# A start-up plan with four places for raw weights, exponentials with running sums on ScalarE, and new planned durations

## The chip, the cores and the metric

The kernel runs on one core of one Trainium2 chip. The metric is the device time of one execution in microseconds (us), as the median of several runs. The profile is of one execution of its own.

## The reference, cut to what matters

Everything is float32 on the inputs' side; the weights arrive as float64 words and are converted on the chip.

```python
# attention in chunks of 32 queries, with 8 memory keys, 16 keys to the left, 8 to the right
scores = scale * np.matmul(q_c, k_full.transpose(0, 1, 3, 2))
scores = scores - np.max(scores, axis=-1, keepdims=True)
a = np.exp(scores)
a = a / (np.sum(a, axis=-1, keepdims=True) + 1e-09)
out[:, :, c_start:c_end] = np.matmul(a, v_full)
...
x = attn_out.transpose(0, 2, 1, 3).reshape(3072, 512)
h = x @ w_in                                  # w_in 512 x 2048
x = (h * (1.0 / (1.0 + np.exp(-1.702 * h)))) @ w_out
h = x @ w_in2
out = (np.maximum(h, 0.0) + alpha * np.minimum(h, 0.0)) @ w_out2
```

## The kernel before, in words

Attention's output is cut into six blocks of 512 tokens. For each block, the first gated layer runs over 16 chunks of 128 hidden units: a product `h` (`mm1`, 12 matmuls of 128x512), a tanh on ScalarE and a multiplication on VectorE (`act1`), a split of the result into a high and a low part (`split_g`, ScalarE then VectorE), and a product into the block's output `ya`/`yb` (`mm2_t`, 12 matmuls). Every matmul operand stands as a high and a low part, so each product is three matmuls. The second layer follows from about 600 us on, and the change does not touch its code.

The change lies in the **start**: block 0. Here three kinds of work run together.

- *First steps* `m` = 0 to 3 (`a_load` ... `a_xpart`): attention for 128 tokens each. TensorE makes the scores `sc`, VectorE the maximum `mx`, the difference, the sum `sm` and the division, ScalarE the exponential between them; then TensorE transposes (`pt`), ScalarE copies (`p`), TensorE multiplies with `v` (`xp`), ScalarE and VectorE write the high and low parts of the block's input `x`.
- *Weights*: 16 chunks of the first layer. `w_load` fetches a chunk's raw words in two DMAs of 512 KB into a tile `wraw`; `w_abs` (ScalarE, L107), `w_bits` 0 to 3 (VectorE, L115, L117, L121, L125), `w_high` (ScalarE, `whi`, L134) and `w_low` (VectorE, `wlo`, L139) turn it into the matmul's two parts. The tile `wtmp` between them has two buffers, so `w_abs` of a chunk waits for `w_low` of the chunk two before it.
- *Double steps* 4 and 6 (`d_load` ... `d_xcopy`): attention for 256 tokens each, for the next block. Their exponentials are already 16 activations of 64 columns with the sum as accumulator (`d_exp`, L414).

What order these have on each engine is set by `emit_jobs`: each piece of work is a `job` with an engine, a planned duration, a rank and its dependencies. A list scheduler takes, again and again, the job that can start earliest (rank decides between equals), and the program is then written out in order of planned start; `keep_in_program_order` (`kp`) fixes that order on every engine and in SyncE's DMA queue. So planned durations are not run times: they decide only who stands before whom. `T_LAND` is what the plan adds after a load, `T_SEM` between engines.

Memory limits the raw weights: before, chunks 0, 1 and 3 to 15 share two places in the pool `wr`, and chunk 2 has one place in the pool `start`. A load of a chunk from 5 on waits until the last reading step (`w_bits` 3, L125) of the chunk two before it is done; chunks 3 and 4 wait for the chunk three before.

Of the kernel before, what the change touches and what calls it, by code (L numbers as in the profile page):

```python
# [56 lines left out]
def fused_kernel(ctx: ExitStack, tc: tile.TileContext, qs, ks, vs, ident, w_in1, w_out1, w_in2, w_out2, alpha, out):  # L57
# [26 lines left out]
    kp = tc.keep_in_program_order  # L84

    def chunk_pool(f):
        return wp if f < NLEFT else side["wp"]

    def w_load(f, half):
        if half == 0:  # L90
            pool = side["start"] if f == 2 else wr
            wst[f] = [pool.tile([128, 2, 512, 2], U32, tag="wraw", name=f"wraw{f}", bufs=1 if f == 2 else 2), None]
        t = wst[f][0]
        if half == 0:
            kp(nc.sync.dma_start(
                out=t[:, 0].rearrange("p n t -> p (n t)").rearrange("p (k f) -> p k f", k=NKC),
                in_=w_in1.bitcast(U32)[:, f * 256:(f + 1) * 256].rearrange("(k p) f -> p k f", p=128),
            ))
        else:
            kp(nc.sync.dma_start(  # L100
                out=t[:, 1].rearrange("p n t -> p (n t)"), in_=w_out1.bitcast(U32)[f * 128:(f + 1) * 128, :],
            ))
# [788 lines left out]

    def emit_jobs():

        free = dict.fromkeys(("pe", "v", "s", "q"), 0.0)
        lag = {"q": T_LAND}
        todo = list(jobs)
        out = []
        while todo:
# [12 lines left out]
        for _, _, j in sorted(out, key=lambda o: o[:2]):  # L911
            j["fn"](*j["args"])
# [56 lines left out]
    for u, m in enumerate((4, 6)):  # L969
        r = DRANK[u]  # L970
        for k, c in enumerate((1.34, 2.2, 2.7)):
            free_ = {0: f"dp{m - 2}", 1: f"dt{m - 2}", 2: f"dp{m - 2}"}[k]
            job(f"dl{m}{k}", "q", c, LOAD_RANK["d"] + 100 * u + k, [free_, f"lv{NSTART - 1}"], d_load, m, k)
        job(f"ds{m}", "pe", 1.5, r, [f"dl{m}0", f"dl{m}1", f"dw{m - 2}1", f"su{NSTART - 2}", f"m1{0}"], d_scores, m)
        job(f"dm{m}", "v", 1.5, r, [f"ds{m}"], d_max, m)
        for k in range(4):
            job(f"de{m}{k}", "s", 1.05, r + 10, [f"dm{m}" if k == 0 else f"de{m}{k - 1}"], d_exp, m, k)
# [3 lines left out]
        job(f"dp{m}", "pe", 2.0, r, [f"dc{m}", f"dl{m}2"], d_pv, m)  # L981
# [93 lines left out]
```

## Time and profile before

| what | value |
|---|---|
| median of 3 runs | 1102.36 us (1102.33 to 1103.25) |
| the profiled execution's own time | 1103.58 us |
| its span, first to last instruction | 1101.8 us |
| mean granted TensorE clock | 0.995 of full speed |
| busy over the span | TensorE 97%, VectorE 69%, ScalarE 37% |
| DMA | 200.22 MB, mean 182 GB/s |

The span is what the trace shows; 1.8 us lie outside it. Busy shares are means over very different stretches. In the page's picture of 40 equal slices, the first slice (27.5 us) has TensorE busy for six tenths, the next three for eight, and nearly all the rest for nine tenths or more. So the start is read by itself, with stretches, waits and engines in order of time. A wait is put down to whatever came last; "issue" is time in which the engine waited for nothing that the profile shows. PE is TensorE, DVE VectorE, ACT ScalarE, SP SyncE, which issues the loads.

### The profile page before, as it was taken

What the parts mean: (1) busy time and instruction counts of PE and PEld (TensorE: products, weight loads), DVE (VectorE), ACT (ScalarE), POOL (GpSimd) and SP (SyncE); (2) the same over time, 40 slices, a digit from 0 to 9 for tenths busy, and PEclk for the clock granted to TensorE, in tenths of its full rate; (3) what the DMA queues carried; (4) which work ended last, traced back from release to release, by engine and by line L of the source; (5) the groups of instructions that cost most, each with busy time, mean ns of one, the idle gap of its engine ahead of it and who ended that gap; (6) DMA issues with size and microseconds to landing.
All of it is one profiled execution on the core that took longest, in us unless ns stands there. A gap on an engine that the chain in (4) does not pass through costs nothing.

```text
span 1101.8 us, 18264 instructions
## 1 busy us (share of the span) xinstructions
PE 1069.9 (97%) x7516; PEld 871.8 (79%) x7516; DVE 762.8 (69%) x1034; ACT 405.1 (37%) x613; POOL 0.2 (0%) x4
## 2 busy tenths in 40 slices
PE   6888999999999999999999999999999999999998
PEld 5776778788888888788778888888888888888886
DVE  6898852667666766666662257798767888677965
ACT  3555432334444343344432222155222345122442
POOL 0000000000000000000000000000000000000000
PEclk9998999999999999999999999999999999999999
DMA  9474612254745555554351066676666867666661
GB/s 350 149 242 146 210 40 90 100 199 158 253 169 208 189 210 194 182 209 157 126 164 65 1 189 189 210 271 211 201 200 194 298 198 220 198 188 214 218 202 58
DMA packets 83619, 200.22 MB, mean 182 GB/s; under 512 B 9041, under 2 KB 25809, under 8 KB 83537
## 3 DMA queue, kind: packets, MB, share of 16 engines
q1 hardware_dynamic: 83536, 199.07, 54.5%
q8 instruction: 59, 0.97, 0.4%
q14 instruction: 24, 0.19, 0.1%
HBM read 157.10 MB, written 41.94 MB: 181 GB/s over the span
## 4 chain that ended last, share of the span: by engine, by line
PE 84%; DVE 7%; DMA 4%; ACT 2%; issue 2%; SPq 1%; DVEq 0%; ACTq 0%
PE h L509 19%; PE accx L810 15%; PE accx L712 12%; PE ya L572 10%; PE yb L572 10%; PE accy L810 6%; PE accy L712 6%; PE hz L712 3%; DMA wraw<-w_out 2%; PE xp L452 1%; PE sc L374 1%; PE pt L436 1%; DVE wtmp L121 1%; DMA k<-ks 1%; DVE wlo L139 1%
## 5 line engine op out<-in xcount | busy, mean ns | idle before, releaser
L509 PE MATMUL h<-x,whi 128*128 128x512 f32 x768 | 242.9, 398 | 3.3 <-ACT whi L134 1.6
L509 PEld LDWEIGHTS h<-x,whi 128*128 128x128 f32 x768 | 145.4, 190 | 36.3 <-ACT whi L134 2.2
L523 DVE SCALAR_TENSOR_TENSOR t<-t,h 128x512 f32<-128x512 f32 x96 | 65.8, 686 | 146.4 <-ACT t L518 146.4
L509 PE MATMUL h<-x,wlo 128*128 128x512 f32 x384 | 152.4, 397 | 2.3 <-DVE wlo L139 2.3
L518 ACT ACTIVATE t<-h 128x512 f32<-128x512 f32 x96 | 57.2, 596 | 169.2 <-PE h L509 169.2
L509 PEld LDWEIGHTS h<-x,wlo 128*128 128x128 f32 x384 | 73.1, 190 | 20.1 <-DVE wlo L139 4.1
L810 PE MATMUL accx<-r,u 128*128 128x512 f32 x360 | 86.5, 396 | 0.0
L564 DVE TENSOR_TENSOR gl<-t,gh 128x512 fp32r<-128x512 f32 x96 | 66.1, 688 | 29.5 <-ACT gh L558 29.5
L712 PE MATMUL accx<-xw,u 128*128 128x512 f32 x240 | 85.8, 390 | 0.3 <-ACT u L695 0.3
L810 PE MATMUL accx<-rx,u 128*128 128x512 f32 x360 | 84.6, 391 | 0.0
L810 PEld LDWEIGHTS accx<-r,u 128*128 128x128 f32 x360 | 67.6, 188 | 16.2
L558 ACT CAST gh<-t 128x512 fp32r<-128x512 f32 x96 | 59.7, 622 | 56.1 <-DVE t L523 52.5
L572 PE MATMUL ya<-gl,whi 128*128 128x512 f32 x192 | 76.5, 398 | 3.4 <-DVE gl L564 3.4
L572 PE MATMUL ya<-gh,whi 128*128 128x512 f32 x192 | 78.4, 408 | 1.3 <-ACT gh L558 1.1
L810 PEld LDWEIGHTS accx<-rx,u 128*128 128x128 f32 x360 | 67.4, 188 | 15.0 <-DVE rx L765 0.5
L572 PE MATMUL yb<-gh,whi 128*128 128x512 f32 x192 | 76.1, 396 | 1.0 <-ACT o L581 0.9
L572 PE MATMUL ya<-gh,wlo 128*128 128x512 f32 x192 | 76.0, 396 | 0.0
L572 PE MATMUL yb<-gl,whi 128*128 128x512 f32 x192 | 75.7, 394 | 0.0
L572 PE MATMUL yb<-gh,wlo 128*128 128x512 f32 x192 | 75.6, 394 | 0.0
L695 ACT COPY s<-accx 128x512 f32<-128x512 f32 x24 | 14.1, 589 | 148.3 <-PE accx L712 148.3
L761 ACT CAST rx<-g 128x1024 fp32r<-128x1024 f32 x42 | 44.3, 1055 | 64.5 <-DVE g L542 24.3
L712 PE MATMUL accx<-xh,u 128*128 128x512 f32 x192 | 67.0, 390 | 0.0
(147 smaller groups left out, 1798.1 us busy)
## 6 DMA issues: line engine op xcount, KB each, us to landing
u<-wo SPq DMA_DIRECT2D x84, 512.0 KB, 4.7
u<-wi SPq DMA_DIRECT2D x72, 512.0 KB, 4.2
v<-vs SPq DMA_DIRECT2D x10, 1024.0 KB, 7.6
k<-ks SPq DMA_DIRECT2D x10, 832.0 KB, 5.3
wraw<-w_in SPq DMA_DIRECT2D x16, 512.0 KB, 5.2
wraw<-w_out SPq DMA_DIRECT2D x16, 512.0 KB, 5.6
raw<-w_in SPq DMA_DIRECT2D x32, 256.0 KB, 3.9
wi<-ob SPq DMA_DIRECT2D x16, 512.0 KB, 4.1
```

The costliest lines, as they stand in the source:

```text
L121: kp(nc.vector.scalar_tensor_tensor(out=a, in0=top, scalar=0xC0000000, in1=a, op0=ALU.bitwise_and, op1=ALU.bitwise_or))
L139: kp(nc.vector.tensor_tensor(out=l, in0=af, in1=h.bitcast(F32), op=ALU.subtract))
L509: pe(nc.tensor.matmul(h[:, :n], w[:, 0, k * 128:(k + 1) * 128], x[:, z, k, :n], start=(i == 0), stop=(i == 3 * NKC - 1)))
L518: mark["s"] = pin(nc.scalar.activation(out=t, in_=h, func=AF.Tanh, scale=1.702 / 2)).ins
L523: mark["v"] = pin(nc.vector.scalar_tensor_tensor(out=t, in0=t, scalar=1.0, in1=h, op0=ALU.add, op1=ALU.mult)).ins
L558: mark["s"] = pin(nc.scalar.copy(gh, g)).ins
L564: mark["v"] = pin(nc.vector.tensor_tensor(out=gl, in0=g, in1=gh.bitcast(F32), op=ALU.subtract)).ins
L572: pe(nc.tensor.matmul(y[m][:, :n], w[:, 1, m * 128:(m + 1) * 128], g[:, :n], start=(f == 0 and i == 0), stop=(f == NF - 1 and i == 2),))
L695: kp(nc.scalar.copy(t, src))
L712: kp(nc.tensor.matmul(to, w[:, c, k * 128:(k + 1) * 128], x[:, k], start=(i == 0 and n not in ADDED), stop=(i == 5), skip_group_check=n in ...
L761: kp(nc.scalar.copy(ring[P, d, jj][0], src))
L810: kp(nc.tensor.matmul(to[:, m], w[:, ft, c, m * 128:(m + 1) * 128], g[:, ft], start=(jj == 0 and ft == 0 and i == 0 and n not in ADDED), s ...
```

## The change

- **Four places.** Chunks 0 to 13 use four places: `f % 4` of 0 or 1 in `wr`, of 2 or 3 in a new pool `boost`. A load waits for the chunk four before it. Chunks 14 and 15 go to `wr` and wait for the chunk two before.
- **Pools.** `start` (the first steps' tiles) is closed after step 3 by a new job `open`; its memory then holds the converted chunks 10 to 13 (`wpb`) and the double steps' tiles. So the double steps' loads wait for the end of the first steps. `boost` is closed at chunk 14, where its memory becomes `wp2`.
- **Exponentials.** `a_sub` and `a_sum` (VectorE) are gone. ScalarE scales the maximum once (`nmx`) and makes 8 activations of 64 columns each, with `nmx` as bias and the sum as accumulator.
- **Durations, ranks, dependencies.** New planned durations, a later `T_LAND`, dependencies looked up when the plan is made, and rank 39 on TensorE for the double steps' scores, transposes and products, ahead of rank 40 of the `y` products.

```diff
-T_LAND = 2.2
-T_SEM = 0.12
-LOAD_RANK = dict(q0=0, q1=1, id=2, v0=3, w0=4, ... w2=11, d=130)
-DRANK = (95, 150)
+T_LAND = 2.7
+T_SEM = 0.15
+LOAD_RANK = dict(q0=0, q1=1, id=2, v0=3, w0=4, ... w2=11, w3=12, d0=105, d1=145)
+DRANK = (110, 160)
...
     def chunk_pool(f):
-        return wp if f < NLEFT else side["wp"]
+        return wp if f < NLEFT else side["wp"] if f >= NF - 2 else side["wpb"]
...
-            pool = side["start"] if f == 2 else wr
-            wst[f] = [pool.tile([128, 2, 512, 2], U32, tag="wraw", name=f"wraw{f}", bufs=1 if f == 2 else 2), None]
+            pool = side["boost"] if f < NF - 2 and f % 4 >= 2 else wr
+            wst[f] = [pool.tile([128, 2, 512, 2], U32, tag="wraw", name=f"wraw{f}", bufs=2), None]
...
-    def a_sub(m):
-        t["ex"] = side["start"].tile([128, 2, 4, KW], F32, tag="ke", name=f"ex{m}", bufs=NSTART)
-        kp(nc.vector.tensor_tensor(out=t["ex"], in0=t["sc"], in1=spread(t["mx"]), op=ALU.subtract))
-    def a_exp(m):
-        kp(nc.scalar.activation(out=ex, in_=ex, func=AF.Exp, scale=1.0 / D ** 0.5))
-    def a_sum(m):
-        kp(nc.vector.tensor_reduce(
-            out=t["sm"].rearrange("p (z n) -> p z n", z=2), in_=t["ex"], axis=mybir.AxisListType.X, op=ALU.add
-        ))
+    def a_exp(m):
+        t = st[m]
+        nmx = side["start"].tile([128, 2 * HP], F32, tag="nmx", name=f"nmx{m}", bufs=2)
+        kp(nc.scalar.mul(nmx, t["mx"], -1.0 / D ** 0.5))
+        t["ex"] = side["start"].tile([128, 2, 4, KW], F32, tag="ke", name=f"ex{m}", bufs=NSTART)
+        for i in range(2 * HP):
+            kp(nc.scalar.activation(
+                out=t["ex"][:, i // 4, i % 4], in_=t["sc"][:, i // 4, i % 4], func=AF.Exp, scale=1.0 / D ** 0.5,
+                bias=nmx[:, i:i + 1], accum_out=t["sm"][:, i:i + 1],
+            ))
...
-    side["start"] = side_stack.enter_context(tc.tile_pool(name="start", bufs=1, side="right"))
-    att_open("at", 1)
+    side["boost"] = side_stack.enter_context(tc.tile_pool(name="boost", bufs=2, side="right"))
+    start_stack = ExitStack()
+    side["start"] = start_stack.enter_context(tc.tile_pool(name="start", bufs=1))
+    def start_done():
+        start_stack.close()
+        side["wpb"] = ctx.enter_context(tc.tile_pool(name="wpb", bufs=1))
+        att_open("at", 1)
...
-        job(f"lw{f}0", "q", 1.35, LOAD_RANK[f"w{f}"] if f < 3 else 100 + 10 * f, [f"b{f - 3}3" if f < 5 else f"b{f - 2}3"] if f > 2 else [], w_load, f, 0)
+        free_ = [f"b{f - 4 if f < NF - 2 else f - 2}3"] if f >= 4 else []
+        job(f"lw{f}0", "q", 1.35, LOAD_RANK.get(f"w{f}", 100 + 10 * f), free_, w_load, f, 0)
...
-        job(f"ex{m}", "s", 0.63, r, [f"su{m}"], a_exp, m)
+        job(f"ex{m}", "s", 2.6, r, [f"mx{m}"], a_exp, m)
...
+    job("open", "q", 0.01, 0, [f"xl{NSTART - 1}"], start_done)
...
-        job(f"m1{f}", "pe", 2.73, 50 + f, ...
+        job(f"m1{f}", "pe", 5.1 if f < 2 else 2.73, 50 + f, ...
...
-        job(f"dt{m}", "pe", 0.8, r, [f"dn{m}"], d_trans, m)
+        job(f"dt{m}", "pe", 0.8, 39, [f"dn{m}"], d_trans, m)
```

Three places show what moves. The first is SyncE's queue of loads from chunk 3's raw weights on, before (`wraw3` is chunk 3; `q4`, `k4`, `v4` are double step 4):

```order
L95 DMA wraw3_427<-w_in1 128x4x256
L100 DMA wraw3_427<-w_out1 128x1024
L355 DMA q4_472<-qs 128x2x512
L359 DMA k4_478<-ks 128x2x832
L363 DMA v4_523<-vs 128x2x1024
L95 DMA wraw4_532<-w_in1 128x4x256
L100 DMA wraw4_532<-w_out1 128x1024
L95 DMA wraw5_601<-w_in1 128x4x256
L100 DMA wraw5_601<-w_out1 128x1024
```

and in the changed kernel:

```order
L95 DMA wraw3_456<-w_in1 128x4x256
L100 DMA wraw3_456<-w_out1 128x1024
L95 DMA wraw4_462<-w_in1 128x4x256
L100 DMA wraw4_462<-w_out1 128x1024
L95 DMA wraw5_520<-w_in1 128x4x256
L100 DMA wraw5_520<-w_out1 128x1024
L351 DMA q4_585<-qs 128x2x512
L355 DMA k4_591<-ks 128x2x832
L359 DMA v4_596<-vs 128x2x1024
L95 DMA wraw6_617<-w_in1 128x4x256
L100 DMA wraw6_617<-w_out1 128x1024
```

Chunks 4 and 5 now stand ahead of the double step's three loads, which stood behind chunk 3 before.

The second is VectorE at first steps 0 and 1, before:

```order
L273 MEMSET sc0_135 64x2x16 x2
L276 TENSOR_REDUCE mx0_172<-sc0_135 128x8
L283 TENSOR_TENSOR ex0_208<-sc0_135,mx0_172 128x512
L276 TENSOR_REDUCE mx1_212<-sc1_175 128x8
L283 TENSOR_TENSOR ex1_215<-sc1_175,mx1_212 128x512
L291 TENSOR_REDUCE sm0_173<-ex0_208 128x8
L296 TENSOR_SCALAR sm0_173<-sm0_173 128x8
L297 RECIPROCAL sm0_173<-sm0_173 128x8
L301 TENSOR_TENSOR ex0_208<-ex0_208,sm0_173 128x512
L291 TENSOR_REDUCE sm1_213<-ex1_215 128x8
L296 TENSOR_SCALAR sm1_213<-sm1_213 128x8
```

and now:

```order
L273 MEMSET sc0_135 64x2x16 x2
L276 TENSOR_REDUCE mx0_172<-sc0_135 128x8
L276 TENSOR_REDUCE mx1_220<-sc1_175 128x8
L292 TENSOR_SCALAR sm0_173<-sm0_173 128x8
L293 RECIPROCAL sm0_173<-sm0_173 128x8
L297 TENSOR_TENSOR ex0_210<-ex0_210,sm0_173 128x512
L292 TENSOR_SCALAR sm1_221<-sm1_221 128x8
L293 RECIPROCAL sm1_221<-sm1_221 128x8
L297 TENSOR_TENSOR ex1_230<-ex1_230,sm1_221 128x512
```

The difference `ex` from `sc` and `mx`, and the sum `sm` from `ex`, are gone from each step.

The third is TensorE around double step 4's transposes (`pt4`; `h1` with `whi1_4` is chunk 4's first product, `ya` and `yb` with `whi1_3` chunk 3's second), before:

```order
L509 MATMUL h1_774<-x0_327,wlo1_4_751 128x512
L436 MATMUL pt4_797<-id_sb_81,ex4_696 128x128 x8
L572 MATMUL ya_675<-gh_794,whi1_3_598 128x512
L572 MATMUL ya_675<-gl_812,whi1_3_598 128x512
L572 MATMUL ya_675<-gh_794,wlo1_3_599 128x512
```

and now:

```order
L568 MATMUL yb_705<-gh_796,whi1_2_588 128x512
L568 MATMUL yb_705<-gl_803,whi1_2_588 128x512
L568 MATMUL yb_705<-gh_796,wlo1_2_589 128x512
L432 MATMUL pt4_860<-id_sb_81,ex4_767 128x128 x8
L505 MATMUL h1_871<-x0_387,whi1_5_771 128x512 x2
L505 MATMUL h1_871<-x0_387,wlo1_5_772 128x512
```

The transposes stood behind chunk 4's `h` and ahead of chunk 3's `y`; they now stand behind chunk 2's `y` and ahead of chunk 5's `h`.

## Rows read from the trace of the kernel before

**Rows 1.** the page's first part: busy us (share of the span), instructions

```profile
PE 1069.9 (97%) x7516; PEld 871.8 (79%) x7516; DVE 762.8 (69%) x1034; ACT 405.1 (37%) x613; POOL 0.2 (0%) x4
```

**Rows 2.** stretches: start:end, length, busy us, granted TensorE clock, DMA share, GB/s

```profile
0.00:35.18 35.18, 21.26 (x557) 17.45 (x557) 25.82 (x44) 13.98 (x19) 0.20 (x4) 1.00 0.94 343
...
36.34:140.67 104.33, 94.25 (x864) 74.56 (x862) 90.40 (x111) 57.00 (x127) 0.00 (x0) 0.95 0.51 169
...
200.00:1102.00 902.00, 894.08 (x5595) 730.48 (x5593) 622.18 (x847) 316.83 (x441) 0.00 (x0) 1.00 0.56 185
```

**Rows 3.** VectorE's waits from 36.34 to 140.67: us in total, times, longest

```profile
DVE wtmp L115 <- ACT wtmp L107: 4.0, 3, 1.6
DVE t L523 <- ACT t L518: 3.9, 4, 2.2
DVE gl L564 <- ACT gh L558: 2.0, 4, 0.7
DVE wlo L139 <- ACT whi L134: 1.7, 2, 1.2
DVE sm L426 <- ACT ex L414: 0.9, 1, 0.9
```

**Rows 4.** VectorE in order of time: start, us, ... [idle before]

```profile
7.22 0.69 DVE L283 TENSOR_TENSOR ex<-sc,mx 128x512 f32<-128x512 f32 x1
...
36.34 1.23 DVE L125 SCALAR_TENSOR_TENSOR wtmp<-wraw,wtmp 128x1024 uint32<-128x1024 uint32 x1
...
139.44 1.23 DVE L139 TENSOR_TENSOR wlo<-wtmp,whi 128x1024 fp32r<-128x1024 f32 x1 [0.51 <-ACT whi L134]
```

**Rows 5.** SyncE queue's longest wait to 150; landing of two kinds of load (page)

```profile
SPq L95 <- DVE wtmp L125: 73.4, 13, 10.2
...
k<-ks SPq DMA_DIRECT2D x10, 832.0 KB, 5.3
...
wraw<-w_out SPq DMA_DIRECT2D x16, 512.0 KB, 5.6
```

**Rows 6.** ScalarE's wait for loads, 36.34 to 140.67

```profile
ACT wtmp L107 <- DMA wraw<-w_out: 10.9, 5, 4.7
```

**Rows 7.** ScalarE in order of time

```profile
7.94 0.63 ACT L287 ACTIVATE ex<-ex 128x512 f32<-128x512 f32 x1 [5.94 <-DVE ex L283]
...
49.42 0.22 ACT L402 ACTIVATE nmx<-mx 128x16 f32<-128x16 f32 x1 [2.91 <-DVE mx L399]
...
50.29 0.31 ACT L414 ACTIVATE ex<-sc,nmx 128x64 f32<-128x64 f32 x1
...
54.83 0.29 ACT L414 ACTIVATION_READ_ACCUMULATOR ex<-sc,nmx 128x1 f32 x1
```

**Rows 8.** TensorE in order of time

```profile
21.07 0.44 PE L259 MATMUL sc<-k,q 64*32 64x64 f32 x8 [1.64 <-issue]
...
35.23 0.79 PE L509 MATMUL h<-x,whi 128*128 128x512 f32 x1 [0.71 <-DVE x L338]
...
45.30 1.48 PE L374 MATMUL sc<-k,q 64*32 64x64 f32 x128
...
49.56 0.39 PE L572 MATMUL ya<-gh,whi 128*128 128x512 f32 x1
...
52.28 0.39 PE L572 MATMUL ya<-gh,whi 128*128 128x512 f32 x1
...
60.45 1.03 PE L436 MATMUL pt<-id_sb,ex 128*128 128x128 f32 x8
...
65.71 2.07 PE L452 MATMUL xp<-p,v 64*64 64x32 f32 x128
...
101.54 1.94 PE L436 MATMUL pt<-id_sb,ex 128*128 128x128 f32 x8 [3.47 <-DVE ex L428]
...
108.05 0.63 PE L509 MATMUL h<-x,whi 128*128 128x512 f32 x2
```

**Rows 9.** the stretch around TensorE's longest wait

```profile
97.94:108.05 10.11, 6.64 (x21) 5.49 (x21) 9.23 (x14) 7.06 (x17) 0.00 (x0) 0.66 0.56 188
```

More of the change, by code (lines that the diff above doesn't have):

```diff
@@ L43 @@
 NLEFT = 10
-T_LAND = 2.2
-T_SEM = 0.12
-LOAD_RANK = dict(q0=0, q1=1, id=2, v0=3, w0=4, q2=5, v1=6, q3=7, v2=8, v3=9, w1=10, w2=11, d=130)
-DRANK = (95, 150)
+T_LAND = 2.7
+T_SEM = 0.15
+LOAD_RANK = dict(q0=0, q1=1, id=2, v0=3, w0=4, q2=5, v1=6, q3=7, v2=8, v3=9, w1=10, w2=11, w3=12, d0=105, d1=145)
+DRANK = (110, 160)
 PREP0 = NF + 5
@@ L129, in w_high @@
     def w_high(f):
-        if f >= NLEFT and "wp" not in side:
+        if f >= NF - 2 and "wp" not in side:
             side_stack.close()
@@ L887, in job @@
     def job(name, eng, cost, rank, deps, fn, *args):
-        j = dict(eng=eng, cost=cost, rank=rank, deps=[by[d] for d in deps if d in by], fn=fn, args=args, end=None)
+        j = dict(eng=eng, cost=cost, rank=rank, deps=deps, fn=fn, args=args, end=None)
         by[name] = j
@@ L897, in emit_jobs @@
         out = []
+        for j in jobs:
+            j["deps"] = [by[d] for d in j["deps"] if d in by]
         while todo:
@@ L934, in fused_kernel @@
     for f in range(NF):
-        job(f"lw{f}0", "q", 1.35, LOAD_RANK[f"w{f}"] if f < 3 else 100 + 10 * f, [f"b{f - 3}3" if f < 5 else f"b{f - 2}3"] if f > 2 else [], w_load, f, 0)
-        job(f"lw{f}1", "q", 1.35, LOAD_RANK[f"w{f}"] if f < 3 else 100 + 10 * f, [f"lw{f}0"], w_load, f, 1)
+        free_ = [f"b{f - 4 if f < NF - 2 else f - 2}3"] if f >= 4 else []
+        job(f"lw{f}0", "q", 1.35, LOAD_RANK.get(f"w{f}", 100 + 10 * f), free_, w_load, f, 0)
+        job(f"lw{f}1", "q", 1.35, LOAD_RANK.get(f"w{f}", 100 + 10 * f), [f"lw{f}0"], w_load, f, 1)
         r = 60 + 10 * f
@@ L940, in fused_kernel @@
             job(f"b{f}{k}", "v", c, r, [f"b{f}{k - 1}" if k else f"wa{f}"], w_bits, f, k)
-        job(f"wh{f}", "s", 1.0, r, [f"b{f}3"], w_high, f)
+        job(f"wh{f}", "s", 1.0, r, [f"b{f}3", "open" if NLEFT <= f < NF - 2 else ""], w_high, f)
         job(f"wl{f}", "v", 1.15, r, [f"wh{f}"], w_low, f)
@@ L944, in fused_kernel @@
     for m in range(NSTART):
-        job(f"lq{m}", "q", 1.76, LOAD_RANK[f"q{m}"], [], a_load, m, 0)
+        job(f"lq{m}", "q", 2.2 if m < 2 else 1.76, LOAD_RANK[f"q{m}"], [], a_load, m, 0)
         job(f"lv{m}", "q", 1.34, LOAD_RANK[f"v{m}"], [f"lq{m}"], a_load, m, 1)
         r = 5 * m
-        job(f"sc{m}", "pe", 1.1, r, [f"lq{m}", f"su{m - 2}"], a_scores, m)
+        job(f"sc{m}", "pe", 1.1, r, [f"lq{m}", f"ex{m - 2}"], a_scores, m)
         job(f"mx{m}", "v", 0.9 if m == 0 else 0.66, r, [f"sc{m}", f"no{m - 2}"], a_max, m)
-        job(f"su{m}", "v", 0.66, r, [f"mx{m}"], a_sub, m)
-        job(f"ex{m}", "s", 0.63, r, [f"su{m}"], a_exp, m)
-        job(f"sm{m}", "v", 0.66, r, [f"ex{m}"], a_sum, m)
-        job(f"in{m}", "v", 0.36, r, [f"sm{m}"], lambda m=m: inv(st[m]))
+        job(f"ex{m}", "s", 2.6, r, [f"mx{m}"], a_exp, m)
+        job(f"in{m}", "v", 0.36, r, [f"ex{m}"], lambda m=m: inv(st[m]))
         job(f"no{m}", "v", 0.66, r, [f"in{m}"], a_norm, m)
@@ L959, in fused_kernel @@
         job(f"xl{m}", "v", 0.66, r, [f"xh{m}"], a_xpart, m, 1)
+    job("open", "q", 0.01, 0, [f"xl{NSTART - 1}"], start_done)
     for f in range(NF):
         r = 30
-        job(f"m1{f}", "pe", 2.73, 50 + f, [f"xl{NSTART - 1}", f"wl{f}", f"tg{f - 2}", f"pc{NSTART - 1}"], m1, f)
+        job(f"m1{f}", "pe", 5.1 if f < 2 else 2.73, 50 + f, [f"xl{NSTART - 1}", f"wl{f}", f"tg{f - 2}", f"pc{NSTART - 1}"], m1, f)
         job(f"th{f}", "s", 0.6, r, [f"m1{f}", f"gl{f - 2}"], th, f)
@@ L972, in fused_kernel @@
             free_ = {0: f"dp{m - 2}", 1: f"dt{m - 2}", 2: f"dp{m - 2}"}[k]
-            job(f"dl{m}{k}", "q", c, LOAD_RANK["d"] + 100 * u + k, [free_, f"lv{NSTART - 1}"], d_load, m, k)
-        job(f"ds{m}", "pe", 1.5, r, [f"dl{m}0", f"dl{m}1", f"dw{m - 2}1", f"su{NSTART - 2}", f"m1{0}"], d_scores, m)
+            job(f"dl{m}{k}", "q", c, LOAD_RANK[f"d{u}"] + k, [free_, "open"], d_load, m, k)
+        job(f"ds{m}", "pe", 1.5, 39, [f"dl{m}0", f"dl{m}1", f"dw{m - 2}1", f"ex{NSTART - 2}", "m10"], d_scores, m)
         job(f"dm{m}", "v", 1.5, r, [f"ds{m}"], d_max, m)
         for k in range(4):
-            job(f"de{m}{k}", "s", 1.05, r + 10, [f"dm{m}" if k == 0 else f"de{m}{k - 1}"], d_exp, m, k)
+            job(f"de{m}{k}", "s", 1.2, r + 10, [f"dm{m}" if k == 0 else f"de{m}{k - 1}"], d_exp, m, k)
         job(f"dn{m}", "v", 1.6, r, [f"de{m}3"], d_norm, m)
-        job(f"dt{m}", "pe", 0.8, r, [f"dn{m}"], d_trans, m)
+        job(f"dt{m}", "pe", 0.8, 39, [f"dn{m}"], d_trans, m)
         job(f"dc{m}", "s", 1.05, r, [f"dt{m}"], d_pcopy, m)
-        job(f"dp{m}", "pe", 2.0, r, [f"dc{m}", f"dl{m}2"], d_pv, m)
+        job(f"dp{m}", "pe", 2.0, 39, [f"dc{m}", f"dl{m}2"], d_pv, m)
         for k in range(2):
```

2 lines of the change are left out of this document (removed).

## The prediction

> **What bounds the kernel now.** I read the page's shares first: TensorE is busy 97% of the span [rows 1]. So time can only come from where TensorE waits or runs slowly. The view by stretches says where that is [rows 2]: from 200 us to the end TensorE is busy 894.1 of 902.0 us. There the change does nothing but swap a few neighbours on VectorE, and I cost that at nothing, since the engine is covered by TensorE there. What is left is the start.
>
> In the start the roles are turned. From 36.34 to 140.67 us VectorE is busy 90.4 of 104.3 us. This stretch begins with the last reading step of chunk 2's weights and ends with the low part of chunk 15, the last piece of the conversion (the rows at 36.34 and 139.44) [rows 4]. Chunk 15's product waits for that piece, and after it TensorE has the rest of that product and two `y` products to do, then works without pause. So **the end of VectorE's conversion sets the end of the start**, and the kernel gets shorter by what this end moves forward.
>
> VectorE's own waits in the stretch sum to 4.0 + 3.9 + 2.0 + 1.7 + 0.9 = 12.5 us [rows 3], so its work there, with the small gaps between instructions, is 104.3 - 12.5 = 91.8 us. The largest wait is for the first ScalarE step of a chunk (L107), and behind that stand loads: ScalarE waits 10.9 us for `wraw` [rows 6]. SyncE's queue shows why a load comes late. It stands 73.4 us in 13 waits until a place is free, that is, until L125 of an earlier chunk is done; only then does the load go out, and it takes 5.6 us to land [rows 5].
>
> **The change, part by part.**
>
> *Exponentials.* VectorE loses eight instructions, a difference and a sum in each of four steps, of 0.69 us each like the row at 7.22 [rows 4]: 5.5 us. ScalarE gets, for one exponential of 0.63 us, a scaled maximum (0.22) and eight short ones. In the double step sixteen such exponentials with their reads of the sum take from 50.29 to 54.83 + 0.29 = 55.12 us, 0.29 us each and 0.2 at the end [rows 7]. So eight take 2.5 us and the step 2.8 with hand-over. ScalarE is busy only 14.0 of the first 35.2 us [rows 2], so 4 x 2.2 us more fits. But the chain of one step gets longer: 2.8 us against three instructions of about 0.65.
>
> I walk the last step, in durations of like rows. The scores of step 3 end at 21.07 + 0.44 = 21.5 us [rows 8]; they hang on loads that do not change, so I keep that. Maximum to 22.2. ScalarE is on the copy of step 2's transposes until 23.2, then 2.8: 26.0. Inverse and division 1.1: 27.1. Transposes 1.1: 28.2. The product of step 2 stands behind them, 1.9, and its copy 0.6: 30.7. VectorE, in its new order, does four weight steps of chunk 1 from 27.7 to 31.5 and only then the low part of step 2: 32.2. Product of step 3 1.9, copy 0.6: 34.7. VectorE finishes two more weight instructions at 35.7 and the last low part at 36.4. Before, TensorE's second `h` matmul, which waits for that part, began at 35.23 [rows 8]: **1.2 us later for TensorE**. But VectorE has then also done the step that it finished at 36.34 before. VectorE is level: the 5.5 us are given back as waits for ScalarE's longer step. The whole part is worth 0.
>
> The Trainium skill, "ScalarE: Activation LUTs", section "What ACT_TABLE_LOAD costs", has a price that speaks against this part: an ACTIVATE whose bias is a pointer costs about 280 ns plus 0.833 ns a column, less 93 ns overlap back to back. By that, an estimate, eight of 64 columns cost 1.9 us against 0.6 for one of 512. The trace agrees on the long one (0.63) [rows 7] and has 2.5 for the eight, since each brings a read of the accumulator; the rows decide. Were it as on the page, the last step would end 0.6 us sooner, and the sum, which hangs on VectorE's end, would be at most 0.6 us lower.
>
> *Places.* A chunk's load now goes out when the chunk four before it is read, for chunks 6 to 13. One chunk costs VectorE 91.8 / 14 = 6.6 us of work in this stretch, so two chunks of advance are some 13 us, against 5.6 for landing [rows 5]. These loads are then early, and 4.0 us of VectorE's waits go [rows 3]. Chunks 14 and 15 keep the rule of two. In my walk chunk 15's load goes out at 117 and lands at 122.5 us, and VectorE wants it at 123.4 after 1.1 of ScalarE: 0.3 us.
>
> *Double step 4's loads* now stand behind chunk 5 and wait for the last product of the first steps, at 34.1. With 5.3 us for `k` [rows 5] and two issues ahead they land at 40.6. TensorE wants them after two `h` products, at 43.9 (36.4 + 2 x 2.72 + 2.1, the loss at the low clock that the 35 matmuls from 35.23 to 45.30 show) [rows 8]. That covers it by 3.3 us; if not, TensorE waits, and it has slack (below). Chunk 6's load behind them in the queue needs L125 of chunk 2 at 37.6 in any case.
>
> *Order and durations.* VectorE's rows from the last step of chunk 2 to the low part of chunk 15 are the same set as before, in another order, so the same 91.8 us. I went through them one by one with the ScalarE and TensorE pieces they wait for. The waits that I find: 0.7 us at the low part of chunk 5, because ScalarE is held by the double step's scaled maximum; 0.8 and 0.4 around double step 6's maximum, for the same reason; the 0.3 above; and 0.3 at chunk 15's high part: 2.5. Such a walk takes every hand-over as exact; I add 0.1 us a chunk, 1.5 for the fourteen: 4.0 us.
>
> *TensorE* must not become the later one. From 36.4 it has 31 products of 12 matmuls, 52.28 - 49.56 = 2.72 us each, two double steps of 1.5 + 0.8 + 2.1, and 2.1 at the low clock: 84.3 + 8.8 + 2.1, ending at 131.6 if it never waits. The walk has it wait 6.5 us, most of it (2.5 us) before `pt4`, which now stands ahead of a product that is ready. A long wait also lowers the clock: after the 3.47 us before 101.54, the transposes and 12 matmuls took until 108.05 [rows 8], 6.5 us for 3.5, and the granted clock of the stretch was 0.66 of full speed [rows 9], part of it at the 1.2 GHz level. One such drop costs 3.0 us and takes the place of later waits.
>
> **The sum.** VectorE's end: 36.4 + 91.8 + 4.0 = 132.2 us, against 140.67: **8.5 us earlier**. The rest of chunk 15's product and two `y` products follow as before. The profiled execution took 1103.6 us, so its like becomes 1095.1. The median of the runs is 1.2 us lower, 1102.4, and becomes 1093.9.
>
> **The rivals.**
>
> 1. *Only the loads' waits go.* The other 8.5 us are waits for tanh and splits, which hang on where TensorE's products stand; the new order may trade some for others. For it: 3.9 and 2.0 us of the waits are of this kind [rows 3]. Against: the walk finds few. Gain 4.0: 1098.4.
> 2. *Nothing.* The waits change their names, or the places don't help because SyncE's queue is in order and loads stand behind double step 6's. Against: in the walk no chunk's load is queued behind a wait that ends later than VectorE's need. 1102.4.
> 3. *Slower: TensorE becomes the bound, at double steps put first.* `pt4`, `pt6` and the two scores now stand ahead of ready products; where their inputs are late, TensorE stands and then runs at the low clock, 3.5 + 3.0 = 6.5 us each [rows 8]. Before, the start's products ended at about 140.7 + 2.3 + 5.4 = 148.4. To be slower by 0.2%, TensorE must lose 148.4 + 2.2 - 131.6 = 19.0 us: three full stalls. Four give 157.6, that is 1111.6; three 1105. I price it at 1106.
> 4. *More.* No waits but the 0.4 us that chunk 15 cannot avoid: 36.4 + 91.8 + 0.4 = 128.6, gain 12.1: 1090.3.
>
> **How the numbers follow.** Forecast 0.58, rival 1 0.17, rival 2 0.11, rival 3 0.09, rival 4 0.05. A measurement here can tell 0.2%, 2.2 us, from no change. Faster: 0.58 + 0.17 + 0.05 = 0.80; same 0.11; slower 0.09. The range leaves out rivals 2 and 3, 0.20 together; it runs from rival 4 at 1090.3 to a little past rival 1, for its own scatter of about 1 us: 1090.3 to 1099.5. The forecast alone covers 1091.5 to 1096.5.
>
> **What would show it.** In the profile after: ScalarE's waits for `wraw` from 36 us on fall from 10.9 to under 3; the low part of chunk 15 on VectorE ends between 130 and 134.5; VectorE's waits before it sum to 2 to 6; the first `h` product starts no earlier than before; TensorE stands 1 to 4 us before `pt4`. From 200 us on nothing differs by more than 2 us. Wrong would be: first steps that end before 34, waits for loads that stay, or TensorE still behind by over 10 us when the last low part is done.

## The result and the profile after

| | before | changed |
|---|---|---|
| median, four runs each, taken together | 1102.39 us | **1092.74 us** (1091.27 to 1093.56) |
| ratio, 95% interval | | 0.9909 [0.9892, 0.9926] |
| the profiled execution's own time, and its span | 1103.58, 1101.8 us | 1093.27, 1091.5 us |

The kernel is 9.7 us faster. The sum had said 8.5 (1093.9).

The first part of the page after shows where work was saved and added (busy us, share, instructions):

```profile
PE 1062.7 (97%) x7516; PEld 868.5 (80%) x7516; DVE 756.8 (69%) x1026; ACT 412.6 (38%) x677; POOL 0.2 (0%) x4
```

Against [rows 1], VectorE has 8 instructions and 6.0 us less, ScalarE 64 instructions and 7.5 us more. TensorE has the same 7516 matmuls. The gain is in when they ran. The view by stretches after, cut at 36.40 us and at the end of chunk 15's low part:

```profile
0.00:36.40 36.40, 20.41 (x557) 16.94 (x557) 21.54 (x36) 22.25 (x83) 0.20 (x4) 0.61 0.88 313
36.40:132.06 95.66, 91.81 (x865) 73.70 (x865) 89.96 (x112) 56.85 (x127) 0.00 (x0) 0.95 0.59 197
200.00:1091.00 891.00, 882.86 (x5436) 722.65 (x5435) 615.98 (x839) 314.77 (x439) 0.00 (x0) 1.00 0.55 186
```

The second line answers to the second of [rows 2]: the same conversion takes 95.7 us instead of 104.3, with VectorE busy for 90.0 (before 90.4). So VectorE's work is nearly the same: of the 8.7 us, 8.2 are time in which it did not work. VectorE's waits in that stretch say which (total us, times, longest):

```profile
DVE t L519 <- ACT t L514: 1.6, 2, 0.8
DVE wlo L139 <- ACT whi L134: 1.4, 3, 0.6
DVE x L466 <- ACT x L464: 0.6, 1, 0.6
DVE wtmp L115 <- ACT wtmp L107: 0.4, 1, 0.4
```

They sum to 4.0 us where [rows 3] had 12.5. The wait at L115, behind which the loads stood, fell from 4.0 to 0.4; the one for tanh from 3.9 to 1.6. In order of time, VectorE's two ends of the stretch and its first reading of block 0's finished output (`o` from `ya`):

```profile
35.91 0.68 DVE L334 TENSOR_TENSOR x<-xp,x 128x512 fp32r<-128x512 f32 x1
36.51 1.22 DVE L125 SCALAR_TENSOR_TENSOR wtmp<-wraw,wtmp 128x1024 uint32<-128x1024 uint32 x1
...
130.83 1.23 DVE L139 TENSOR_TENSOR wlo<-wtmp,whi 128x1024 fp32r<-128x1024 f32 x1 [0.52 <-ACT whi L134]
...
148.08 0.68 DVE L579 TENSOR_SCALAR o<-ya 128x512 f32<-128x512 f32 x1
```

The last low part ends at 130.83 + 1.23 = 132.06 us; before it was 140.67 [rows 4]. Block 0's output was first read at 156.74 us before:

```profile
156.74 0.68 DVE L583 TENSOR_SCALAR o<-ya 128x512 f32<-128x512 f32 x1
```

It is read at 148.08 now, 8.66 earlier. This last row is the end of the start, and the experiments are read by it too.

### The profile page after: what moved, and what is told of

It reads as the page before. It is cut to its first block, busy times and chain, and to the rows that moved or that the text cites. A ratio compares the mean times of both kernels' runs of the same rounds, so it can differ in the third digit from the quotient of the medians.

```text
span 1091.5 us, 18327 instructions
## 1 busy us (share of the span) xinstructions
PE 1062.7 (97%) x7516; PEld 868.5 (80%) x7516; DVE 756.8 (69%) x1026; ACT 412.6 (38%) x677; POOL 0.2 (0%) x4
## 4 chain that ended last, share of the span: by engine, by line
PE 79%; DVE 11%; DMA 5%; issue 3%; ACT 2%; SPq 1%; DVEq 0%; ACTq 0%
PE h L505 16%; PE accx L806 15%; PE accx L708 12%; PE yb L568 8%; PE ya L568 8%; PE accy L806 6%; PE accy L708 6%; PE hz L708 3%; PE xp L448 2%; DMA wraw<-w_out 1%; DVE wtmp L125 1%; DVE wtmp L121 1%; DVE gl L560 1%; DVE wlo L139 1%; DMA wi<-oa 1%
```

## The experiments

In every traced kernel I cut the start at three places. A is where TensorE's second `h` product begins (35.23 before, 36.65 after): the first steps are over. B is the end of the low part of chunk 15 on VectorE. C is VectorE's first row that reads block 0's output. The waits are VectorE's from 36.4 us to B. All ratios are against the kernel before, which ran beside each group. Kernels 1 to 8 change what the plan is made from, so each differs in order too, and not only in its edit.

| kernel | A | B | C | waits | median us | ratio [95%] |
|---|---|---|---|---|---|---|
| before | 35.23 | 140.67 | 156.74 | 12.5 | 1102.4 | 1 |
| changed | 36.65 | 132.06 | 148.08 | 4.0 | 1092.7 | 0.9909 [0.9892, 0.9926] |
| 1 without four places | 36.17 | 134.96 | 148.25 | 6.2 | 1092.7 | 0.9906 [0.9890, 0.9923] |
| 2 old exponentials | 34.36 | 138.91 | 152.22 | 9.0 | 1098.3 | 0.9956 [0.9939, 0.9972] |
| 3 old numbers | 36.98 | 131.98 | 147.78 | 4.2 | 1094.1 | 0.9917 [0.9902, 0.9932] |
| 4 places alone | 36.05 | 132.47 | 146.41 | 3.6 | 1091.1 | 0.9889 [0.9873, 0.9905] |
| 5 pools alone | 35.16 | 139.22 | 155.22 | 11.1 | 1099.3 | 0.9968 [0.9955, 0.9980] |
| 6 numbers alone | 34.35 | 137.09 | 150.38 | 7.9 | 1095.4 | 0.9931 [0.9919, 0.9943] |
| 7 old rank on TensorE | 36.13 | 123.91 | 166.02 | 2.2 | 1110.6 | 1.0073 [1.0058, 1.0089] |
| 8 more work on VectorE | 37.42 | 143.70 | 157.01 | 4.2 | 1102.3 | 0.9997 [0.9987, 1.0008] |
| 9 before, alpha later | 36.80 | 140.45 | 156.52 | 10.7 | 1101.8 | 0.9997 [0.9987, 1.0007] |
| 10 as 2, alpha later | 34.42 | 136.66 | 149.97 | 6.7 | 1095.4 | 0.9956 [0.9941, 0.9970] |
| 11 changed, alpha later | 36.15 | 130.21 | 146.20 | 2.9 | 1091.6 | 0.9910 [0.9897, 0.9922] |
| 12 as 4, once more | 35.00 | 131.00 | 144.96 | 3.2 | 1090.8 | 0.9909 [0.9894, 0.9924] |

Kernels 4 and 12 are the same, and 9 does not differ from before until 118 us; yet A differs by 1.05 and 1.57 us within these pairs. So one profile's A is no better known than that, and differences between C's of 1 to 2 us decide nothing alone.

**1. Without four places.** The rule for raw weights is the old one (chunk 2 in a place of its own, the others in two); exponentials, numbers and pools stay as changed.

```diff
-            pool = side["boost"] if f < NF - 2 and f % 4 >= 2 else wr
+            pool = side["boost"] if f == 2 else wr
-        free_ = [f"b{f - 4 if f < NF - 2 else f - 2}3"] if f >= 4 else []
+        free_ = ([f"b{f - 3}3"] if f < 5 else [f"b{f - 2}3"]) if f > 2 else []
```

> The changed kernel with the raw weights' places as before (chunk 2 alone in its place, all others in two). Theory, that the load waits are about half of the gain and the order the rest: loads go out only when the chunk two before is read, ScalarE's waits for wraw from 36 us on come back to 8 to 11 us, VectorE's last low part of chunk 15 ends 4 to 6 us later than 132.1, and the time is 1096.5 to 1098.7. Rival A, that the order alone made the gain and the places are slack: under 1094.5. Rival B, that the places are all of it: 1101 or more.

The time did not change at all, where 1096.5 to 1098.7 was expected. The trace shows why it could not be read from VectorE's waits alone. In this kernel they are 2.2 us more, and ScalarE again waits for loads, 12.2 us in 7 (against 3.5 in 2 after):

```profile
DVE wlo L139 <- ACT whi L134: 3.8, 4, 1.2
DVE wtmp L115 <- ACT wtmp L107: 1.9, 2, 1.2
DVE gl L560 <- ACT gh L554: 0.5, 1, 0.5
```

```profile
ACT wtmp L107 <- DMA wraw<-w_out: 12.2, 7, 2.5
```

B is 2.9 us later, but the plan, made anew, had also moved TensorE's products: behind the last low part stands only `h15` (the order is `y12 y13 y14 h15`), in the changed kernel `h15 y13 y14`. From B to C it takes 13.29 us instead of 16.02. The start of `h15` on TensorE:

```profile
137.46 0.63 PE L505 MATMUL h<-x,whi 128*128 128x512 f32 x2
```

That is 2.5 us after B, with no idle time before it, and from 34 to 160 us no wait of TensorE is put down to a low part in this kernel. So here B does not set the end of the start. The places' share in this plan is nothing, and the end of VectorE's conversion is not the whole of the end: what TensorE has left at that moment counts with it.

**2. Old exponentials.** `a_sub`, one activation of 512 columns, `a_sum`, as before; all else as changed.

```diff
-        job(f"ex{m}", "s", 2.6, r, [f"mx{m}"], a_exp, m)
-        job(f"in{m}", "v", 0.36, r, [f"ex{m}"], lambda m=m: inv(st[m]))
+        job(f"su{m}", "v", 0.66, r, [f"mx{m}"], a_sub, m)
+        job(f"ex{m}", "s", 0.63, r, [f"su{m}"], a_exp, m)
+        job(f"sm{m}", "v", 0.66, r, [f"ex{m}"], a_sum, m)
+        job(f"in{m}", "v", 0.36, r, [f"sm{m}"], lambda m=m: inv(st[m]))
```

> The changed kernel with the first steps' difference and sum back on VectorE and one exponential of 512 columns. Theory, that this part is worth 0, since VectorE's saving comes back as waits for the longer step: 1090.5 to 1095.0, first h product at most 1.5 us earlier, VectorE's end of chunk 15's low part within 2 us of 132.1. Rival, that the 5.5 us which VectorE saves are real: 1097 to 1099.

It is 5.5 us slower than the changed kernel. Its time is the rival's (1097 to 1099), not the theory's; but the rows show another cause than the rival's. From 36.4 us to B VectorE takes 102.5 us: 9.0 of waits (after: 4.0) and 93.5 of work (91.7), so 5.0 and 1.8 more; behind B 2.7 less (one multiplication by the tanh and one split, behind B in the changed kernel, stand ahead of it here). That is the 4.1 us by which C is later. The waits are the larger part, and they are for loads:

```profile
DVE wtmp L115 <- ACT wtmp L107: 4.1, 2, 3.0
DVE wlo L139 <- ACT whi L134: 2.9, 4, 1.2
DVE t L523 <- ACT t L518: 2.0, 2, 1.7
```

```profile
118.89 1.12 ACT L107 ACTIVATE wtmp<-wraw 128x1024 f32<-128x1024 f32 x1 [4.61 <-DMA wraw<-w_out]
127.92 1.12 ACT L107 ACTIVATE wtmp<-wraw 128x1024 f32<-128x1024 f32 x1 [5.93 <-DMA wraw<-w_out]
```

These are chunks 14 and 15, the two that kept the rule of two places. So, by these rows, what this edit cost is for the most part where the new plan then happened to put their loads, not the exponentials.

**3. Old numbers.** `T_LAND`, `T_SEM`, load ranks, `DRANK`, planned durations and the double steps' rank on TensorE as before; places, pools and exponentials as changed.

```diff
-T_LAND = 2.7
+T_LAND = 2.2
...
-        job(f"dt{m}", "pe", 0.8, 39, [f"dn{m}"], d_trans, m)
+        job(f"dt{m}", "pe", 0.8, r, [f"dn{m}"], d_trans, m)
```

> The changed kernel with the planned durations, ranks, landing and hand-over allowances of before; four places and the new exponentials stay (the plan knows these still take 2.6 us). Theory, that the order is the other half of the gain: VectorE's waits for tanh and splits come back in part, its last low part ends 3 to 5 us after 132.1, time 1095.7 to 1097.7. Rival, that the places alone made the gain and the numbers nothing: under 1094.5.

No difference that these runs can tell: 0.9917 against 0.9909, intervals overlapping, C within 0.3 us. The expected loss (1095.7 to 1097.7) did not come.

**4 to 6. One part at a time.** Kernel 5 has only the new pools, the `open` job and the dependencies looked up when the plan is made, 4 has these and the four places, 6 these and the new numbers. Each is the changed kernel with the edits of 1, 2 and 3 combined: 1 + 2 + 3, 2 + 3, 1 + 2. The new exponentials alone with the pools were not run.

> The new places and pools with the exponentials and the plan's numbers of before. Theory, that the places give the loads' share: 1097.0 to 1099.5, ScalarE's waits for wraw after 36 us under 3 us, VectorE's waits for tanh and splits 5 us or more. Rival, that the places give all: under 1094.5; rival, that without the new numbers they give nothing: 1101 or more.

> The new pools alone: places for raw weights, exponentials and the plan's numbers as before, but the first steps' pool closed after step 3, so that the double steps' loads wait for that; TensorE's order of products is that of the kernel before. Theory, that four places alone gain the whole under the old numbers, as the run with only the places said: 1100.5 to 1104. Rival, that moving the double step's loads behind the weights' loads is what helped in all runs so far: under 1097.

> The new pools and the new planned numbers and ranks, with places and exponentials as before. Theory, that the numbers gain something by themselves but leave waits for loads: 1096 to 1100, VectorE's last low part 135 to 138. Rival A, that the numbers alone do it: under 1094.5. Rival B, that they do nothing without places or the new exponentials: 1101 or more.

The pools alone give 3.1 us. From there the **places give 8.2 us** (0.9968 to 0.9889, intervals apart; to the 0.9909 of kernel 12, the same program, it is 6.5 us), though undoing them in experiment 1 cost nothing. The new numbers in place of them give 3.9. VectorE's waits of kernel 5 and of kernel 4:

```profile
DVE wtmp L115 <- ACT wtmp L107: 4.3, 2, 2.7
DVE t L523 <- ACT t L518: 2.2, 4, 0.8
DVE gl L564 <- ACT gh L558: 2.0, 4, 0.7
DVE wlo L139 <- ACT whi L134: 1.7, 2, 1.2
DVE sm L426 <- ACT ex L414: 0.9, 1, 0.9
```

```profile
DVE wlo L139 <- ACT whi L134: 1.1, 1, 1.1
DVE t L523 <- ACT t L518: 1.1, 2, 0.9
DVE gl L564 <- ACT gh L558: 1.1, 2, 0.6
DVE sm L426 <- ACT ex L414: 0.3, 1, 0.3
```

Kernel 5 has nearly the rows of before [rows 3], but for the tanh's, 2.2 us where 3.9 was. With the places the wait at L115 is gone, and the waits for tanh and splits are halved with it, though nothing was done for them. ScalarE is no longer held by loads (11.2 us in kernel 5, 0.3 in kernel 4), so it can come to them sooner; that this alone does it is not shown, since the order on TensorE differs too. The waits for loads go as the prediction had it, and the gain is more than its price of 4.0 us.

None of the six times from experiment 1 to 6 fell into the range that its theory gave: what one part is worth was not foreseen once.

**7. Old rank on TensorE.** Only the rank 39 of the double steps' scores, transposes and products is taken back.

```diff
-        job(f"ds{m}", "pe", 1.5, 39,
+        job(f"ds{m}", "pe", 1.5, r,
-        job(f"dt{m}", "pe", 0.8, 39,
+        job(f"dt{m}", "pe", 0.8, r,
-        job(f"dp{m}", "pe", 2.0, 39,
+        job(f"dp{m}", "pe", 2.0, r,
```

> The changed kernel with the double steps' ranks on TensorE as before (DRANK 110 and 160, behind all products); all else as changed. The plan then puts both double steps behind nearly all products, and the next block's input, which they make, is late. Theory: TensorE stands 10 to 16 us at the start's end for double step 6's chain of scores, maximum, exponentials, division, transposes and products: 1102 to 1109, though VectorE's last low part ends by 131. Rival, that the rank is worth nothing: under 1095.

VectorE is through with the weights at 123.91 us, earliest of all, and the kernel is the slowest. The double steps slip behind the `y` products to the very end of the start, and there TensorE finds nothing ready. TensorE in order of time:

```profile
136.07 2.04 PE L370 MATMUL sc<-k,q 64*32 64x64 f32 x128 [4.03 <-DMA q<-qs]
146.71 1.94 PE L432 MATMUL pt<-id_sb,ex 128*128 128x128 f32 x8 [8.60 <-DVE ex L424]
149.76 3.64 PE L448 MATMUL xp<-p,v 64*64 64x32 f32 x128 [1.10 <-ACT p L437]
154.59 0.80 PE L505 MATMUL h<-x,whi 128*128 128x512 f32 x1 [1.19 <-ACT x L464]
```

Four waits of 14.9 us, and the work between them at up to 1.8 times its duration (`xp` 3.64 us, 2.07 in [rows 8]), at a granted clock of 0.50 from 136 to 161 us. B to C is 42.1 us here, and the time is a little above the 1102 to 1109 expected. TensorE is the bound at a double step, as in rival 3, but from the opposite side: there the double steps stand too early, here too late. The new rank keeps this away under the new numbers; kernels 3, 4 and 5, with the old numbers, have the old rank too and no such end (B to C 13.9 to 16.0 us).

**8. More work on VectorE.** `w_low` of chunks 3 to 10 is written twice: eight instructions of 1.22 us more, the plan told of it.

```diff
-        kp(nc.vector.tensor_tensor(out=l, in0=af, in1=h.bitcast(F32), op=ALU.subtract))
+        for _ in range(2 if 3 <= f <= 10 else 1):
+            kp(nc.vector.tensor_tensor(out=l, in0=af, in1=h.bitcast(F32), op=ALU.subtract))
```

> The changed kernel with the low part of chunks 3 to 10 written twice on VectorE: 8 more instructions of 1.15 us, 9.2 us of work with no new data. Theory, that VectorE's end sets the end of the start: its last low part ends 6.5 to 9.2 us later and the time is 1098.5 to 1102. Rival, that TensorE sets it and VectorE has slack: under 1096.

A pair takes 2.40 us from its start to the next instruction's, a single one 1.14; so each added one costs some 1.25 us, and all eight 10.0:

```profile
45.26 2.48 DVE L140 TENSOR_TENSOR wlo<-wtmp,whi 128x1024 fp32r<-128x1024 f32 x2
47.66 0.68 DVE L561 TENSOR_TENSOR gl<-t,gh 128x512 fp32r<-128x512 f32 x1
```

These 10.0 us of work made the kernel 9.6 us slower and C 8.9 us later. B is 11.6 us later, more than the 6.5 to 9.2 expected, and behind it TensorE has 2.7 us less to do, as in kernel 1. TensorE waits where VectorE's low parts come late (in the changed kernel one such wait of 0.5 us):

```profile
PE h L506 <- DVE wlo L140: 6.1, 6, 1.4
```

So in the changed kernel more work on VectorE lengthens the start nearly one for one. That less work would shorten it as much is not shown: TensorE is busy for 91.8 of the 95.7 us from 36.4 to B.

**9 to 11. Alpha's load.** In experiment 2 the trace showed one thing more. SyncE's queue there:

```profile
113.99 0.47 SPq L1008 DMA_DIRECT2D al_sb<-alpha  x1
119.05 4.08 SPq L95 DMA_DIRECT2D wraw<-w_in  x1
```

Alpha is 8 KB, but 2048 pieces of 4 bytes. It is needed only by the second layer, yet stands right ahead of chunk 15's load, whose issue takes 4.08 us instead of 0.37. Before, the same pair stands at 120.86 and takes 3.34; in the changed kernel alpha is ahead of chunk 14's load, 1.40. Kernels 9, 10 and 11 are the kernel before, kernel 2 and the changed one with alpha behind chunk 15:

```diff
+            with tc.issue_after(side["last_load"].ins):
-            kp(nc.sync.dma_start(out=al_sb, in_=alpha.rearrange("(f p) -> p f", p=128)))
+                kp(nc.sync.dma_start(out=al_sb, in_=alpha.rearrange("(f p) -> p f", p=128)))
```

> The kernel before, with one load moved: alpha (8 KB, 2048 pieces of 4 bytes), which stands directly ahead of chunk 15's raw weights in SyncE's queue, goes behind them. In the trace of before the issue of the DMA behind alpha takes 3.34 us, where the same one takes 0.37 elsewhere. Theory A: alpha's pieces hold up the next issue. Then chunk 15's first issue takes 0.4 us, ScalarE's wait of 4.7 us for it falls to about 1.7, VectorE's wait of 1.55 us before the clamp of chunk 15 goes, its last low part ends at about 139.1 instead of 140.7, and the time is 1.5 us lower: 1100.9 (1100.0 to 1101.5). Rival B: the issue is held by the 1.5 MB of double step 8's loads ahead of it, not by alpha: the issue still takes over 2 us and the time stays at 1102.4.

> The changed kernel with the old exponentials (1098.3 in its own run), and alpha's load moved behind chunk 15's raw weights. In that run the issue behind alpha took 4.08 us, ScalarE then waited 5.93 us for chunk 15 and VectorE 3.00. Theory A (alpha holds up the issue): issue 0.4, ScalarE's wait about 2.3, VectorE's 0; last low part at about 135.9 instead of 138.9, time about 1095.3 (1094.3 to 1096.3): over half of what undoing the exponentials cost was a load's place in a queue, not the exponentials. Rival B (the loads of double step 8 do): 1098.3, unchanged.

> The changed kernel, with alpha's load moved behind chunk 15's raw weights. There alpha stands ahead of chunk 14's, whose first issue takes 1.40 us. Theory A: issue 0.4, ScalarE's wait of 0.88 us for chunk 14 and VectorE's of 0.37 go; the last low part ends about 0.4 us earlier, at 131.7; time 1092.3 (1091.7 to 1092.8). Rival B: 1092.7, unchanged. The two are close here; the wait for chunk 14 tells them apart, not the time.

SyncE's queue at chunk 15 in kernel 10, and ScalarE's wait for that chunk:

```profile
120.17 0.37 SPq L95 DMA_DIRECT2D wraw<-w_in  x1
120.59 0.49 SPq L100 DMA_DIRECT2D wraw<-w_out  x1
121.13 0.51 SPq L1009 DMA_DIRECT2D al_sb<-alpha  x1
```

```profile
126.92 1.13 ACT L107 ACTIVATE wtmp<-wraw 128x1024 f32<-128x1024 f32 x1 [5.34 <-DMA wraw<-w_out]
```

The issue that stood behind alpha takes 0.37 us in all three: alpha did hold it. The time is another matter. In kernel 9 ScalarE's wait for chunk 15 falls from 4.72 to 3.02 us, and VectorE's 1.55 us behind it go, but the wait for chunk 14 grew (VectorE's from 0.91 to 2.04); the time is the same. In kernel 11 the wait for chunk 14 did not go as theory A had it (1.17 us, was 0.88), and the time is not told apart. In kernel 10 ScalarE's wait falls only from 5.93 to 5.34 and C is 2.25 us earlier; its median is 2.9 us lower, as theory A said, but its 12 runs lie between 1094.6 and 1103.3 and the ratio is that of experiment 2. So alpha is worth 0 to 3 us, open beyond that. In kernel 10 ScalarE still waits 5.34 us, since chunk 15's load goes out at 120.17, when chunk 13 has been read: the rule of two places.

**12. Places alone, once more.**

> The four places and the new pools with the old exponentials and the old plan's numbers, once more, beside the changed kernel with alpha moved. Its alpha stands behind chunk 15 already. Theory: it repeats its 1091.1 (1090.4 to 1091.5) and stays about 1 us below the changed kernel, since its last low part ends 0.4 us later but only h15 and two y products are left. Rival: the difference of the first runs was scatter, and both come out within 0.5 us.

Ten runs of this kernel in two groups have medians of 1091.1 and 1090.8, under the 1092.7 of the changed one. But the second group's ratio is 0.9909, the same as the changed kernel's, so that it beats it is not shown. It is as fast, and it does without the new exponentials and the new numbers.

## Why the prediction was right, and which steps of it were not

**The bound.** Right for the changed kernel. VectorE's end came at 132.06 us where 132.2 was written, and experiment 8 shows that work added on VectorE counts nearly one for one (8.9 us of C for 10.0). It holds for this order and not for every one: in kernel 1 TensorE reaches chunk 15's product 2.5 us after VectorE is done.

**The sum.** 91.8 us of work was 91.7; 4.0 of waits was 4.0. The end of the first steps was written as 36.4 and is 35.91 + 0.68 = 36.59. The sum gave 8.5; C came 8.66 earlier. That it is this close is in part luck, since A alone differs by 1.05 and 1.57 us between two traces of one start. The waits one by one, in order of time, are these and the 0.52 us at 130.83 shown above:

```profile
57.56 1.23 DVE L139 TENSOR_TENSOR wlo<-wtmp,whi 128x1024 fp32r<-128x1024 f32 x1 [0.63 <-ACT whi L134]
71.66 0.69 DVE L519 SCALAR_TENSOR_TENSOR t<-t,h 128x512 f32<-128x512 f32 x1 [0.79 <-ACT t L514]
74.11 1.29 DVE L466 TENSOR_TENSOR x<-xp,x 128x512 fp32r<-128x512 f32 x2 [0.62 <-ACT x L464]
88.36 0.69 DVE L519 SCALAR_TENSOR_TENSOR t<-t,h 128x512 f32<-128x512 f32 x1 [0.77 <-ACT t L514]
89.29 1.23 DVE L139 TENSOR_TENSOR wlo<-wtmp,whi 128x1024 fp32r<-128x1024 f32 x1 [0.25 <-ACT whi L134]
118.47 0.69 DVE L115 TENSOR_SCALAR wtmp<-wtmp 128x1024 f32<-128x1024 f32 x1 [0.37 <-ACT wtmp L107]
```

Five of the seven are the walk's, at its places or one chunk off: 0.63 at chunk 5's low part (0.7 written), 0.77 and 0.25 behind double step 6's maximum (0.8 and 0.4), 0.37 for a late load (0.3) and 0.52 at chunk 15's end (0.3), 2.5 us as written. The other two, 1.41 us, are not in the walk. They fill the allowance of 1.5, which was meant for hand-overs; that it fits is luck.

The two profiled executions differ by 10.3 us, 1.7 of it behind C: from there to the end of the span it is 945.1 us before, 943.4 after, and between 941 and 945 in the fourteen traces of the table, in no order that goes with the edits. That is scatter, not gain.

**The exponentials at nothing.** As a statement on VectorE's place at 36.4 us it held. VectorE is busy 21.54 us in the first 36.4, 5.46 less than the 27.00 before, so the 5.5 us saved were given back as waits; its last step of chunk 2 begins at 36.51, before at 36.34 [rows 4]. TensorE's second `h` begins 1.4 us later (1.2 written). ScalarE's first step:

```profile
7.07 0.21 ACT L283 ACTIVATE nmx<-mx 128x8 f32<-128x8 f32 x1 [5.06 <-DVE mx L276]
7.31 0.32 ACT L286 ACTIVATE ex<-sc,nmx 128x64 f32<-128x64 f32 x1
7.53 0.19 ACT L286 ACTIVATION_READ_ACCUMULATOR ex<-sc,nmx 128x1 f32 x1
7.62 0.31 ACT L286 ACTIVATE ex<-sc,nmx 128x64 f32<-128x64 f32 x1
...
9.55 0.24 ACT L286 ACTIVATION_READ_ACCUMULATOR ex<-sc,nmx 128x1 f32 x1
```

From 7.07 to 9.79 it is 2.7 us, 2.8 written, and the starts of the exponentials are 0.28 to 0.31 apart. By the Trainium skill, "ScalarE: Activation LUTs", section "What ACT_TABLE_LOAD costs", it would be 0.24 each, an estimate. The rows have more, with a read of the accumulator of 0.19 to 0.24 us behind each; that the read makes the difference is likely, not shown by a run without it. But as a statement on the part's **worth in the whole** the step failed: with the rest of the change in place, undoing it costs 5.5 us (experiment 2), and with the old numbers it costs nothing (experiment 4, if anything faster than 3).

**The places at 4.0.** As a reading of the trace it held: the wait at L115 fell from 4.0 to 0.4. As a share it failed both ways: 0 when undone (experiment 1), 8.2 when added to the old numbers (4 against 5; 6.5 by the ratio of kernel 12). The step assumed that the parts of the change add up, each worth the waits that bear its name. The runs show that they stand in for each other: 1, without the places, and 4, with the places alone, are both as fast as the whole. Why is in part open. Every such edit gives the scheduler another order; in kernel 1 the order puts other products where the changed kernel has chunk 15's, and so its later B costs nothing.

**Double step 4 and TensorE.** The walk had 2.5 us of waiting before `pt4`; it is 2.05:

```profile
65.49 1.69 PE L432 MATMUL pt<-id_sb,ex 128*128 128x128 f32 x8 [2.05 <-DVE ex L424]
66.83 1.20 PE L505 MATMUL h<-x,whi 128*128 128x512 f32 x2
```

The transposes then took 1.69 us for 1.03 and a pair of matmuls 1.20 for 0.63 [rows 8]. The 12 matmuls from 66.83 to 70.86 took 4.0 us for 2.72. The granted clock from 65.49 to 70.86 us was 0.68 of full speed, and 1.00 in the pieces before the wait and after. So that drop cost 2.0 us, less than the 3.0 written. It was put at nothing, since TensorE had slack; it was not free. VectorE's two waits at 71.66 and 74.11 are for ScalarE, and ScalarE waited for just these products of TensorE:

```profile
71.03 0.60 ACT L514 ACTIVATE t<-h 128x512 f32<-128x512 f32 x1 [1.73 <-PE h L505]
73.00 1.07 ACT L464 CAST x<-xp 128x512 fp32r<-128x512 f32 x2 [1.37 <-PE xp L448]
```

By these rows 1.41 us of the 4.0 that VectorE waits come from this stretch, from `pt4` standing ahead of a product that was ready.

**Chunks 14 and 15.** Written as 0.3 us of waiting on VectorE for chunk 15; measured 0.37 for chunk 14 and nothing for chunk 15, though ScalarE's waits for loads are 3.5 us, a little over the 3 that were set as the mark. Their loads go out late, and here little hangs on it. In kernels 2 and 10 it does.

**The rivals.** Rival 3, TensorE standing at double steps put first, did not come in the changed kernel; that TensorE can become the bound at a double step experiment 7 shows, at 1110.6 us, with the double steps last. Rival 1, only the loads' waits, fell: tanh's fell too, as kernels 4 and 5 show by themselves. Rival 4 was nearly met in number by kernels 4 and 12, at 1091.1 and 1090.8 (1090.3 written), but not by its mechanism: they have 3.6 and 3.2 us of waits, not 0.4.

## What to carry to other kernels

Where a planner sets the order, find the engine that sets the end of the stretch, and forecast its end as start plus work plus the waits found by a walk through the new order: that sum came out within 0.2 us, closer than two traces of one kernel agree. Do not price the parts of such a change one by one by the waits that carry their names, since each part moves the whole order, and what a part is worth depends on which others are there; measure a part both by taking it from the new kernel and by adding it to the old. And beside the last engine's end, ask what the other engine has left to do at that moment: in kernel 1, 2.7 us less of it made up for an end 2.9 us later.

## What was not expected of the hardware

A load of 8 KB in 4-byte pieces made the next load in SyncE's queue take 3.34 and 4.08 us to issue, and 1.40 in the changed kernel, against 0.37 where alpha had been moved away; alpha itself needs 6.5 us to land in the changed kernel. Alpha is not the only cause of a slow issue: in kernel 9, with alpha gone from there, the 1 MB load of `v` behind chunk 14 took 2.57 us to issue, where the kernel before has 0.45.

The granted clock of the first 36.4 us is 0.61 in the changed kernel's rows and 1.00 before [rows 2], yet the same 557 matmuls were busy for 20.41 us and 21.26 before. Nor does it go with the program: kernel 11 has the changed kernel's start and reads 1.00, kernel 9 has the start of before and reads 0.60, each over its first 36.4 us. So in this stretch, where TensorE works in short bursts, I would not read a difference of this column as a loss.
